# Output products in four 32-row tiles, half of their evictions split over two engines, and a list scheduler that writes the whole order

## The chip, the cores and the metric

One NeuronCore of a Trainium2 chip runs the whole program. The metric is the device time of one execution in microseconds (us), lower is better. Five engines work side by side, each through its own instructions strictly in the order in which the program lists them: PE (TensorE, matrix products; PEld is its loading of the stationary operand), DVE (VectorE), ACT (ScalarE), POOL (GpSimd) and SP, which here only starts DMA transfers. An instruction whose input is not there, or whose output buffer is not free yet, holds up everything behind it on its engine.

## What is computed

```python
# x: 4 x 12480 x 128, inducing: 32 x 128, w_in: 128 x 2048, w_out: 2048 x 128
def mab(q, kv):
    s = scale * (q @ kv.transpose(0, 2, 1))
    s = s - s.max(-1, keepdims=True)
    a = np.exp(s)
    a /= a.sum(-1, keepdims=True) + 1e-09
    return a @ kv
h = mab(I, x)          # 32 rows per batch, from all 12480 rows of x
y = mab(x, h)          # every row of x attends to those 32 rows
g = y @ w_in
out = np.maximum(0.01 * g, g) @ w_out
```

## The kernel before

The kernel has two paths. The one that runs, `fixed_sign_path`, uses that the rows of `h` differ little, so that every hidden unit has one sign for the whole batch. Then the two weight matrices fold with `h` into one 32 x 128 matrix M per batch, and the output is the attention weights of a row times M. A flag, computed at the end, says whether this held; the other path, which is as it was, would follow if not.

The 12480 rows of a batch are six groups of 2048 rows (J = 4 parts of 32 rows x K = 16) and a remainder of 192 rows, `RG`. There are four batches, so 24 groups and 4 remainders. Each group goes through two passes.

First pass: `load` brings 1 MB of x into `xr` (6 buffers). `turn` transposes it on PE in four quarters into `xT_ps` and copies each to `xT`. `first_scores` multiplies by the 32 inducing rows into `s_ps` and reads that out as `e`, with maxima. A step is two groups: `maxima` sets the shift, `weigh` takes the exponential (ACT) and transposes it to `ay` (DVE), `values` sums on PE into `h_ps`, `gather` adds that up.

Between the passes of a batch there is a chain: `inverse`, `normalise`, `hidden` (`H_ps`, `HT`), the leak on POOL (`G`), `fold` (`m_ps`), `spread` (`M_ps`). M is copied into `blocks`, block by block, so that 64 rows of the array serve two of the four parts J at a time: 64 x 258, which is two blocks of 128 columns and two columns of ones for the sums.

Second pass: `second_scores` (`s_ps` again) finds the largest magnitude (`low`), spreads it over the partitions with one more product (`low_ps`, `least`) and takes the exponential into `uT`. `output` then runs four times per group, once per quarter: two products of 64 rows x 258 columns into two banks of `po`, then on DVE the sums plus 1e-9 (`inv`, L1754), a reciprocal (L1755), and one multiplication that also moves 128 x 512 values to `osb` (L1756). `store` sends `osb` (2 buffers) out in four transfers of 256 KB.

PSUM has eight banks: `tp` (transposes and small products) two, `sc` (scores) one, `hp` (sums of values, and `m_ps`) one, `po` two buffers of two banks.

A loop over stages `s` writes the program: stage s transposes group s, takes the scores of s - 1, the second scores of s - 8, and the output of s - 9. The order on each engine is not quite that of the code, since the framework's own scheduler reorders what is written outside `manual_schedule`. In the fp32 products of the profile a matrix product is two MATMUL instructions, a transposition is one.

Of the kernel before, what the change touches and what calls it, by code (L numbers as in the profile page):

```python
# [11 lines left out]
I32 = mybir.dt.int32  # L12
# [1369 lines left out]

@with_exitstack
def fixed_sign_path(
# [33 lines left out]

    const = ctx.enter_context(tc.tile_pool(name="fconst", bufs=1))
# [12 lines left out]
    def value_ps(name):  # L1432
        return ps_h.tile([P, P], F32, tag="hp", name=name)

    def small(name, n=1, bufs=2):
        return sb.tile([P, n], F32, tag=name, name=name, bufs=bufs)
# [9 lines left out]
    blocks = [const.tile([P, 2 * P + 2], F32, tag=f"blocks{i}", name=f"blocks{i}") for i in range(2)]  # L1446
# [5 lines left out]
    hTs, sums_of, absolute, outs = {}, {}, {}, {}  # L1452
# [5 lines left out]
    def words(w):  # L1458
        return w.bitcast(I32).rearrange("p (n t) -> p n t", t=2)

    def setup():
# [13 lines left out]
        for blk in blocks:  # L1475
            nc.gpsimd.memset(blk, 0.0)
            for j in range(4):
                nc.gpsimd.memset(blk[32 * j : 32 * j + 32, 2 * P + j % 2 : 2 * P + j % 2 + 1], 1.0)
# [8 lines left out]
    def load(b, g, pieces=1):  # L1487
        J, K, rows, w = size(g)
        if g == RG:
            t = sb.tile([P, K, C], F32, tag="xrr", name="xrr", bufs=2)  # L1490
        else:
            t = sb.tile([P, K, C], F32, tag="xr", name="xr", bufs=6)
        src, n = rows_of(b, g), K // pieces
        for i in range(pieces):
            nc.sync.dma_start(t[:rows, n * i : n * i + n, :], src[:, n * i : n * i + n, :])
        xr[b, g] = t

    raws = []

    def load_weights(i):  # L1500
        raw = sb.tile([P, TOK, 2], I32, tag="osb", name="raw", bufs=2)
# [7 lines left out]
        raws.append(raw)  # L1509

    def convert(i):
        raw = raws[i]
        a = sb.tile([P, TOK], I32, tag="cv_a", name="cv_a", bufs=2)
        sign = sb.tile([P, TOK], I32, tag="cv_b", name="cv_b", bufs=1)
        tail = sb.tile([P, TOK], I32, tag="uT", name="cv_t", bufs=3)
        nc.scalar.mul(a.bitcast(F32), raw[:, :, 1].bitcast(F32), 2.0**-112)
        nc.vector.tensor_scalar(
            out=sign, in0=raw[:, :, 1], scalar1=-0x80000000, scalar2=None, op0=ALU.bitwise_and
        )
        nc.vector.scalar_tensor_tensor(  # L1520
            out=a, in0=a, scalar=3, in1=sign, op0=ALU.logical_shift_left, op1=ALU.bitwise_or
        )
        nc.scalar.mul(tail, raw[:, :, 0].bitcast(U32), 2.0**-29)
        if i < 4:
            dst, shape = w_in_sb[:, i].rearrange("p k r -> p r k").bitcast(I32), "p (r k) -> p r k"
            dst, a, tail = dst, a.rearrange(shape, k=16), tail.rearrange(shape, k=16)
# [4 lines left out]
    def turn(b, g, q, copy):  # L1531
        J, K, rows, w = size(g)
        n = min(K, 4)
        if q == 0:
            if g == RG:
                xT[b, g] = sb.tile([P, K, rows], F32, tag="xTr", name="xTr", bufs=3)
            else:
                xT[b, g] = sb.tile([P, K, rows], F32, tag="xT", name="xT", bufs=9)
        pt = turn_ps("xT_ps")
# [399 lines left out]
```

## Time and profile before

| | |
|---|---|
| device time, median of 3 runs | 373.02 us (372.03 to 373.57) |
| device time of the profiled execution | 367.05 us |
| its span, first to last instruction | 365.2 us |
| granted TensorE clock over the span | 0.867 of 2.4 GHz |
| moved by DMA | 55.80 MB, 153 GB/s over the span |

The profiled execution was 6 us shorter than the median of the timed ones. The profile's times are counted from the first instruction of the span. Busy times of an engine are the union of its instructions' times; a PE instruction's end is modelled, so the time from one product to the next is a better measure of PE than its length.

### The profile page before, as it was taken

Reading aid. Unit: us, or ns where it says so; the run is one execution under the profiler, and the core shown is the slowest. Engines: PE = TensorE matmul, PEld = TensorE weight load, DVE = VectorE, ACT = ScalarE, POOL = GpSimd, SP = SyncE. Lnnn points to the kernel's source line nnn. Section 1 sums busy time; section 2 is a strip of 40 time slices with the busy share of each in tenths; the row PEclk is TensorE's granted clock in tenths of the full one; section 3 lists DMA queues with packets and bytes.
Section 4 is the critical chain, followed back from the end, with each engine's and each line's share of the span. In section 5 each row is a group of like instructions: output and inputs, shape, how many; then the busy total and the mean of one; then the engine's idle time right before and its main releaser. Section 6 shows DMA issues by size and latency. Waiting matters only on the chain.

```text
span 365.2 us, 5886 instructions
## 1 busy us (share of the span) xinstructions
PE 277.1 (76%) x2275; PEld 144.0 (39%) x2275; DVE 189.4 (52%) x609; ACT 105.0 (29%) x221; POOL 17.1 (5%) x32
## 2 busy tenths in 40 slices
PE   4575968799989788887978886778977677685660
PEld 3343635455535353353534451433432222232420
DVE  1235553548555654546565744526754455646670
ACT  2454663535333351332422432041200100001000
POOL 2113230100000000000001000000001000000000
PEclk9679689999999999999987999898985598787555
DMA  7976685154582644048924096233613146356565
GB/s 237 426 270 191 213 300 188 56 226 120 128 278 58 151 196 118 0 117 325 290 88 117 7 260 206 44 83 79 156 32 83 37 120 150 79 133 149 126 162 115
DMA packets 20724, 55.80 MB, mean 153 GB/s; under 512 B 2352, under 2 KB 3536, under 8 KB 17872
## 3 DMA queue, kind: packets, MB, share of 16 engines
q1 hardware_dynamic: 20640, 55.32, 51.4%
q8 instruction: 20, 0.33, 0.4%
q14 instruction: 16, 0.13, 0.1%
q10 hardware_dynamic: 48, 0.02, 0.0%
HBM read 29.77 MB, written 25.56 MB: 152 GB/s over the span
## 4 chain that ended last, share of the span: by engine, by line
PE 60%; DVE 22%; ACT 6%; issue 4%; DMA 2%; SPq 1%; POOL 1%; DVEq 0%; POOLq 0%; ACTq 0%
PE s_ps L1549 18%; PE po L1748 16%; PE xT_ps L1541 10%; PE h_ps L1633 8%; DVE osb L1756 7%; DVE low L1720 4%; ACT xT L1544 4%; PE low_ps L1724 3%; DVE e L1566 2%; DMA raw<-in_moe_w_in_dram 2%; DVE ay L1610 2%; PE H_ps L1672 1%; DVE inv L1754 1%; PE m_ps L1695 1%; PE mx_ps L1582 1%
## 5 line engine op out<-in xcount | busy, mean ns | idle before, releaser
L1748 PE MATMUL po<-blocks,uT 64*128 64x258 f32 (+1 forms) x400 | 81.8, 497 | 27.3 <-DVE osb L1756 18.6
L1541 PE MATMUL xT_ps<-ident,xr 128*128 128x128 f32 x384 | 64.5, 309 | 7.3 <-ACT xT L1544 7.0
L1544 ACT COPY xT<-xT_ps 128x512 f32<-128x512 f32 x96 | 53.6, 585 | 53.5 <-PE xT_ps L1541 52.7
L1756 DVE TENSOR_TENSOR osb<-po,inv 128x512 f32<-128x512 f32 (+1 forms) x100 | 67.1, 686 | 1.9
L1748 PEld LDWEIGHTS po<-blocks,uT 64*128 64x128 f32 (+1 forms) x400 | 38.9, 217 | 73.0 <-issue 33.1
L1541 PEld LDWEIGHTS xT_ps<-ident,xr 128*128 128x128 f32 x384 | 47.9, 157 | 25.6 <-ACT xT L1544 14.3
L1735 ACT ACTIVATE uT<-s_ps,least 128x512 f32<-128x512 f32 (+1 forms) x28 | 17.8, 634 | 99.7 <-PE po L1748 51.4
L1549 PE MATMUL s_ps<-xT,hT 128*32 128x512 f32 x192 | 41.3, 644 | 4.2 <-DVE e L1566 3.1
L1754 DVE TENSOR_SCALAR inv<-po 128x4 f32<-128x4 f32 (+1 forms) x100 | 15.5, 155 | 42.7 <-PE po L1748 42.4
L1549 PE MATMUL s_ps<-xT,indT 128*32 128x512 f32 x192 | 32.5, 628 | 6.3 <-ACT xT L1544 5.9
L1566 DVE TENSOR_SCALAR_CACHE_REDUCE e<-s_ps 128x512 f32<-128x512 f32 (+1 forms) x28 | 17.4, 621 | 38.1 <-PE s_ps L1549 38.0
L1633 PE MATMUL h_ps<-xr,ay 128*32 128x128 f32 x768 | 32.6, 287 | 1.8 <-DVE ay L1610 1.7
L1633 PEld LDWEIGHTS h_ps<-xr,ay 128*32 128x32 f32 x768 | 24.3, 114 | 12.0 <-issue 7.4
L1720 DVE TENSOR_REDUCE low<-s_ps 128x1 f32<-128x512 f32 (+1 forms) x28 | 17.4, 623 | 19.9 <-PE s_ps L1549 19.9
L1724 PE MATMUL low_ps<-ident,low 128*128 128x128 f32 x56 | 14.9, 351 | 12.3 <-DVE low L1720 9.8
L1606 ACT ACTIVATE e<-e,nm 128x512 f32<-128x512 f32 (+1 forms) x28 | 18.3, 655 | 10.9 <-DVE nm L1585 10.9
L1724 PEld LDWEIGHTS low_ps<-ident,low 128*128 128x128 f32 x56 | 9.1, 204 | 28.9 <-DVE low L1720 21.0
L1610 DVE STREAM_TRANSPOSE ay<-e 128x512 f32<-128x512 f32 (+1 forms) x28 | 17.0, 626 | 5.0 <-ACT e L1606 5.0
L1755 DVE RECIPROCAL inv<-inv 128x4 f32<-128x4 f32 (+1 forms) x100 | 17.3, 173 | 2.3
L1601 ACT ACTIVATE al<-nm 128x1 f32<-128x1 f32 x8 | 2.4, 294 | 39.7 <-DVE lower L1587 36.6
L1726 DVE TENSOR_REDUCE least<-low_ps 128x1 f32<-128x128 f32 x28 | 8.0, 286 | 11.0 <-PE low_ps L1724 11.0
L1549 PEld LDWEIGHTS s_ps<-xT,hT 128*32 128x32 f32 x192 | 6.0, 111 | 15.6 <-DVE e L1566 6.4
(84 smaller groups left out, 138.6 us busy)
## 6 DMA issues: line engine op xcount, KB each, us to landing
out_dram<-osb SPq DMA_DIRECT2D x96, 256.0 KB, 4.4
xr<-in_x_dram SPq DMA_DIRECT2D x22, 1024.0 KB, 8.0
xr<-in_x_dram SPq DMA_DIRECT2D x8, 256.0 KB, 5.0
raw<-in_moe_w_in_dram SPq DMA_DIRECT2D x4, 512.0 KB, 8.6
raw<-in_moe_w_out_dram SPq DMA_DIRECT2D x4, 512.0 KB, 4.2
xrr<-in_x_dram SPq DMA_DIRECT2D x4, 96.0 KB, 8.3
out_dram<-osb SPq DMA_DIRECT2D x8, 48.0 KB, 1.7
ind<-in_inducing_dram ACTq DMA_DIRECT2D x1, 16.0 KB, 3.1
```

Source lines behind the costliest of these rows:

```text
L1541: nc.tensor.transpose(pt[:, k * rows : (k + 1) * rows], xr[b, g][:rows, 4 * q + k, :], ident[:rows, :rows])
L1544: copy(xT[b, g][:, 4 * q : 4 * q + n, :].rearrange("p k t -> p (k t)"), pt[:, : n * rows])
L1549: nc.tensor.matmul(ps[32 * j : 32 * j + 32, :w].rearrange("p (k r) -> p k r", r=32), lhsT, xT[b, g][:, :, 32 * j : 32 * j + 32], start=Tru ...
L1566: nc.vector.tensor_scalar(out=e[:rows], in0=sp[:rows, :w], scalar1=1.0, scalar2=None, op0=ALU.mult, op1=ALU.max, accum_out=rm[:rows],)
L1606: nc.scalar.activation(e[:rows, :w], e[:rows, :w], AF.Exp, bias=nm[:rows], scale=SCALE, accum_out=zg[:rows])
L1610: nc.vector.transpose(t[:rows].rearrange("p k m -> p (k m)"), e[:rows, :w])
L1633: nc.tensor.matmul(hp[32 * (k % 4) : 32 * (k % 4) + 32, :], t[:rows, k, :], rows_in[:rows, k, :], start=(i == 0 and k < 4), stop=(last[k % ...
L1720: nc.vector.tensor_reduce(out=low[:rows], in_=ps[:rows, :w], op=ALU.max, axis=AX.X, apply_absolute_value=True, negate=True)
L1724: nc.tensor.matmul(pl[:, :P], low.broadcast_to([P, P]), ident, start=True, stop=True)
L1748: nc.tensor.matmul(po[:m, h, : 2 * P + 2], part, blocks[b % 2][64 * h : 64 * h + 64, :], start=True, stop=True, tile_position=(64 * h, 0),)
L1754: nc.vector.tensor_scalar_add(inv2[:m], po[:m, :, 2 * P :][:, :, :2], 1e-9)
L1756: nc.vector.tensor_tensor(out=osb[:m, :, kk, :].rearrange("p (h j) c -> p h j c", h=2), in0=po[:m, :, : 2 * P].rearrange("p h (j c) -> p h ...
```

## The change

The formulas, the groups, the two passes and the transfers' sizes stay. Four things change.

1. `output` works on half a group with four tiles of 32 rows. M is copied once (`folded`, 128 x 129 with one column of ones) instead of four times, and every part J is a row tile of its own that writes into its own bank. A half group is 8 products of 32 rows x 129 columns, in four banks. `po` is now one buffer of four banks.
2. `inverses` takes the sums of a half group at once (128 x 8). `divided` evicts a half group in two pieces of 128 x 512: one is scaled on DVE as before, the other (`BY_COPY`) is copied unscaled by ACT and then multiplied in place by POOL.
3. `Plan` orders everything. Every piece of work is added with the engines that may do it, an estimated length, what it follows, the buffers that it takes and uses, and a rank. The scheduler repeatedly picks what can start soonest, and writes the program in the order of the starts that it worked out, under `manual_schedule`, so the framework does not reorder. A transposed quarter may be copied by ACT or by DVE, whichever the plan finds free.
4. The banks are dealt anew: `tp` two, `sc` two, `po` four; the sums of values and `m_ps` now take a `tp` buffer. `e` gets 4 buffers instead of 3, the weights have buffers of their own instead of those of `osb`.

```diff
+class Plan:
+    HANDOVER, LANDING, SWITCH, NEAR, STICK = 0.12, 2.0, 0.12, 0.1, 0.4
+    def ordered(self):
...
+                    at = max([free[engine]] + [from_op(a, engine) for a in after])
...
+                    start, order_rank = at, rank
+                    if mode is not None and mode != last_mode:
+                        start, order_rank = at + self.SWITCH, rank + self.STICK
+                    choices.append((start, order_rank, name, engine, length))
+            soonest = min(choices)
+            same = [c for c in choices if c[3] == soonest[3] and c[0] <= soonest[0] + self.NEAR]
+            start, _, name, engine, length = min(same, key=lambda c: (c[1], c[0], c[2:4]))
...
+    BY_COPY = ((0, 1), (1, 1))
-    ps_s = ctx.enter_context(tc.tile_pool(name="fps_s", bufs=1, space=bass.MemoryType.PSUM))
-    ps_h = ctx.enter_context(tc.tile_pool(name="fps_h", bufs=1, space=bass.MemoryType.PSUM))
-    ps_o = ctx.enter_context(tc.tile_pool(name="fps_o", bufs=2, space=bass.MemoryType.PSUM))
+    ps_s = ctx.enter_context(tc.tile_pool(name="fps_s", bufs=2, space=bass.MemoryType.PSUM))
+    ps_o = ctx.enter_context(tc.tile_pool(name="fps_o", bufs=1, space=bass.MemoryType.PSUM))
...
-        po = ps_o.tile([P, 2, TOK], F32, tag="po", name="po")
-        for h in range(2):
-            part = t[64 * h : 64 * h + 64, n * kk : n * kk + n, :].rearrange("p k r -> p (k r)")
-            nc.tensor.matmul(
-                po[:m, h, : 2 * P + 2], part, blocks[b % 2][64 * h : 64 * h + 64, :],
-                start=True, stop=True, tile_position=(64 * h, 0),
-            )
+        V["po", b, g, h] = po = ps_o.tile([P, 4, TOK], F32, tag="po", name="po")
...
+        for i in range(n):
+            flat = t.rearrange("p k r -> p (k r)")[:, m * (n * h + i) : m * (n * h + i) + m]
+            for j in range(J):
+                part = slice(32 * j, 32 * j + 32)
+                nc.tensor.matmul(
+                    po[:m, j, (P + 1) * i : (P + 1) * (i + 1)], flat[part], folded[b % 2][part, :],
+                    start=True, stop=True, tile_position=(32 * j, 0),
+                )
...
+        if step == "copy":
+            nc.scalar.copy(dst, src)
+            return
+        scale = inv[:m, j0:j1, :n].unsqueeze(3).broadcast_to([m, j1 - j0, n, C])
+        engine = nc.vector if step == "whole" else nc.gpsimd
+        engine.tensor_tensor(out=dst, in0=src if step == "whole" else dst, in1=scale, op=ALU.mult)
...
+            add(("C", b, g, q), {"ACT": 0.6 * f, "DVE": 0.7 * f}, lambda e, q=q: turned(b, g, q, e),
...
+    for emit in plan.ordered():
+        emit()
```

What this does to the order on PE is seen at two places. The names are those of the section on the kernel; `po` is the output product, `mx_ps` the product of `maxima`, and a row with xN is N products in a row. First, PE in the second half of the program, where both passes run. Before:

```order
L1748 MATMUL po<-blocks_84,uT 128x258 x8
L1549 MATMUL s_ps<-xT,indT 32x512
L1748 MATMUL po<-blocks_84,uT 128x258 x4
L1549 MATMUL s_ps<-xT,indT 32x512 x3
L1748 MATMUL po<-blocks_84,uT 128x258 x2
L1549 MATMUL s_ps<-xTr,indT 32x64 x3
L1748 MATMUL po<-blocks_84,uT 128x258 x2
L1582 MATMUL mx_ps<-rd,e_78 128x12
L1549 MATMUL s_ps<-xT,hT 32x512
L1748 MATMUL po<-blocks_84,uT 128x258 x2
```

And now, at a like place:

```order
L1863 MATMUL po<-folded_84,uT 128x129 x8
L1607 MATMUL xT_ps<-ident,xr 128x128 x12
L1863 MATMUL po<-folded_84,uT 128x129 x8
L1832 MATMUL low_ps<-ident,low 128x128
L1607 MATMUL xT_ps<-ident,xr 128x128 x4
L1627 MATMUL s_ps<-xT,indT 32x512 x4
L1607 MATMUL xT_ps<-ident,xr 128x128 x8
L1863 MATMUL po<-folded_84,uT 128x129 x8
L1665 MATMUL mx_ps<-rd,e_77 128x8
L1607 MATMUL xT_ps<-ident,xr 128x128 x8
L1627 MATMUL s_ps<-xT,hT 32x512 x4
```

Score products were cut in two by output products; now the four products of a group stand together, and transpositions stand between the halves of an output.

Second, PE from the last sum of values (`h_ps`) of the last batch on. Before:

```order
L1633 MATMUL h_ps<-xrr,ay 32x128 x2
L1652 MATMUL z_ps<-zn,e_78 128x1
L1549 MATMUL s_ps<-xT,hT 32x512
L1662 MATMUL hT_ps<-folds,hs 128x64
L1549 MATMUL s_ps<-xT,hT 32x512 x3
L1724 MATMUL low_ps<-ident,low 128x128
L1748 MATMUL po<-blocks_84,uT 128x258 x6
L1549 MATMUL s_ps<-xTr,hT 32x64 x3
L1748 MATMUL po<-blocks_84,uT 128x258 x2
L1724 MATMUL low_ps<-ident,low 128x128
L1672 MATMUL H_ps<-w_in_sb,hT 32x512 x4
L1549 MATMUL s_ps<-xT,hT 32x512 x4
```

And now (`z_ps`, `hT_ps`, `H_ps`, `m_ps` and `M_ps` are the products of the chain between the passes):

```order
L1723 MATMUL h_ps<-xrr,ay 32x128 x2
L1742 MATMUL z_ps<-zn,e_77 128x1
L1863 MATMUL po<-folded_83,uT 128x129 x8
L1755 MATMUL hT_ps<-folds,hs 128x64
L1766 MATMUL H_ps<-w_in_sb,hT 32x512 x4
L1627 MATMUL s_ps<-xT,hT 32x512 x4
L1863 MATMUL po<-folded_83,uT 64x129 x3
L1627 MATMUL s_ps<-xT,hT 32x512 x4
L1799 MATMUL m_ps<-w_out_sb,G 32x128 x16
L1832 MATMUL low_ps<-ident,low 128x128
L1810 MATMUL M_ps<-mc,e_77 128x128
```

Between the first product of the chain, `z_ps`, and `H_ps` stood eight output products of the batch before (four quarters), the second scores of a group and of a remainder, and three small products; now one half group and `hT_ps` stand there. From the last sum of values to the end the list before has the output of 38 quarters and two remainders; the list now has that of 13 halves and two remainders.

Third, PE at the very end. Before:

```order
L1724 MATMUL low_ps<-ident,low 128x128
L1748 MATMUL po<-blocks_85,uT 128x258 x6
L1549 MATMUL s_ps<-xTr,hT 32x64 x3
L1748 MATMUL po<-blocks_85,uT 128x258 x2
L1724 MATMUL low_ps<-ident,low 128x128
L1799 MATMUL v_ps<-ones,each 1x1
L1748 MATMUL po<-blocks_85,uT 128x258 x20
L1748 MATMUL po<-blocks_85,uT 64x258 x2
```

And now:

```order
L1832 MATMUL low_ps<-ident,low 128x128
L1863 MATMUL po<-folded_84,uT 128x129 x8
L1627 MATMUL s_ps<-xTr,hT 32x64 x3
L1832 MATMUL low_ps<-ident,low 128x128
L1863 MATMUL po<-folded_84,uT 128x129 x8
L1927 MATMUL v_ps<-ones,each 1x1
L1863 MATMUL po<-folded_84,uT 128x129 x48
L1863 MATMUL po<-folded_84,uT 64x129 x3
```

Before, ten quarters of two and a half groups and the remainder stood behind the last small product; now six halves, three groups, stand there in one run, each of which takes the only `po` buffer.

## Rows read from the trace of the kernel before

**Rows 1.** The page's head and part 1: busy time per engine, with shares of the span.

```profile
span 365.2 us, 5886 instructions
...
PE 277.1 (76%) x2275; PEld 144.0 (39%) x2275; DVE 189.4 (52%) x609; ACT 105.0 (29%) x221; POOL 17.1 (5%) x32
```

**Rows 2.** Windows: busy time (and count) per engine, PE's granted clock, DMA share, GB/s.

```profile
0.00:62.00 62.00, 42.05 (x386) 27.31 (x386) 24.59 (x67) 31.04 (x63) 12.58 (x26) 0.83 0.72 257
62.00:264.00 202.00, 170.55 (x1598) 90.50 (x1597) 112.30 (x375) 67.85 (x146) 3.43 (x5) 0.97 0.49 143
264.00:286.00 22.00, 15.07 (x89) 5.98 (x88) 11.12 (x38) 1.72 (x5) 1.05 (x1) 0.67 0.21 50
286.00:356.00 70.00, 49.41 (x204) 20.26 (x204) 41.43 (x131) 4.43 (x7) 0.00 (x0) 0.72 0.52 124
356.00:365.20 9.20, 0.00 (x0) 0.00 (x0) 0.00 (x0) 0.00 (x0) 0.00 (x0) 0.50 0.51 116
```

**Rows 3.** Groups on PE from 62 to 264 us: busy us, mean ns | idle before.

```profile
L1748 PE MATMUL po<-blocks,uT 64*128 64x258 f32 (+1 forms) x240 | 45.3, 452 | 9.8 <-DVE osb L1756 6.5 <-DVE inv L1754 3.3
L1549 PE MATMUL s_ps<-xT,hT 128*32 128x512 f32 x136 | 23.7, 603 | 3.1 <-DVE e L1566 3.1
```

**Rows 4.** Waits of PE from 62 to 264 us: total us, times, longest.

```profile
PE po L1748 <- DVE osb L1756: 6.5, 9, 1.2
PE low_ps L1724 <- DVE low L1720: 6.5, 14, 0.8
PE s_ps L1549 <- DVE e L1566: 3.4, 7, 0.8
```

**Rows 5.** Chain that ended last: start us, length us, what and how many instructions.

```profile
97.76 1.04 PE xT_ps L1541 x8
...
167.41 0.73 PE po L1748 x4
...
171.09 1.07 PE po L1748 x8
...
228.69 2.00 PE h_ps L1633 x64
...
286.25 1.26 PE po L1748 x4
```

**Rows 6.** Groups by form, whole span: busy us, mean ns | idle before.

```profile
L1756 DVE TENSOR_TENSOR osb<-po,inv 128x512 f32<-128x512 f32 x96 | 64.4, 687 | 1.9
L1544 ACT COPY xT<-xT_ps 128x512 f32<-128x512 f32 x96 | 53.6, 585 | 53.5 <-PE xT_ps L1541 52.7
L1541 PEld LDWEIGHTS xT_ps<-ident,xr 128*128 128x128 f32 x384 | 47.9, 157 | 25.6 <-ACT xT L1544 14.3 <-issue 8.5 <-DVE least L1726 1.3
...
L1755 DVE RECIPROCAL inv<-inv 128x4 f32<-128x4 f32 x96 | 16.7, 174 | 2.2
...
L1754 DVE TENSOR_SCALAR inv<-po 128x4 f32<-128x4 f32 x96 | 14.9, 155 | 41.8 <-PE po L1748 41.5
...
L1687 POOL TENSOR_TENSOR G<-HT,slope 128x512 f32<-128x512 f32 x4 | 4.2, 1047 | 161.2 <-DVE both L1781 117.6 <-DVE slope L1682 43.6
```

**Rows 7.** Instructions in order of time, 34.8 to 36.5 us: start, length, engine.

```profile
35.12 1.27 POOL L1529 TENSOR_TENSOR w_in_sb<-cv_a,cv_t 128x512 int32<-128x512 int32 x1 [0.69 <-DVE cv_a L1520]
...
35.62 0.80 DVE L1575 TENSOR_TENSOR rd<-rm,own 128x8 f32<-128x8 f32 x1
```

**Rows 8.** The instructions on tile rd: duration ns min/median/max.

```profile
L1575 DVE TENSOR_TENSOR rd<-rm,own x12: 155/167/795, 21.5 to 257.8; 128x8 f32<-128x8 f32 x8, 128x12 f32<-128x12 f32 x4
```

**Rows 9.** The chain again, from the last sum of values to the end.

```profile
262.93 0.80 PE h_ps L1633 x24
...
274.39 1.98 PE H_ps L1672 x8
...
355.18 0.68 DVE osb L1756
```

**Rows 10.** DMA issues of the page: KB each, median us to landing.

```profile
out_dram<-osb SPq DMA_DIRECT2D x96, 256.0 KB, 4.4
xr<-in_x_dram SPq DMA_DIRECT2D x22, 1024.0 KB, 8.0
```

More of the change, by code (lines that the diff above doesn't have):

```diff
@@ L1459, in words, with copying @@
         return w.bitcast(I32).rearrange("p (n t) -> p n t", t=2)
+    def copying(engine):
+        return nc.scalar.copy if engine == "ACT" else nc.vector.tensor_copy
     def setup():
@@ L1474, in setup @@
         )
[L1475 to L1478, printed above, removed]
+        for f in folded:
+            nc.gpsimd.memset(f, 1.0)
         pt = turn_ps("ind_ps")
@@ L1485, in rows_of, with load @@
         return x[b][at : at + 32 * J * K, :].rearrange("(p k) c -> p k c", k=K)
-    def load(b, g, pieces=1):
+    def load(b, g, i, pieces):
         J, K, rows, w = size(g)
[L1489 to L1498, printed above, removed]
+        if i == 0:
+            if g == RG:
+                xr[b, g] = sb.tile([P, K, C], F32, tag="xrr", name="xrr", bufs=2)
+            else:
+                xr[b, g] = sb.tile([P, K, C], F32, tag="xr", name="xr", bufs=BUFS["xr"])
+        t, src, n = xr[b, g], rows_of(b, g), K // pieces
+        nc.sync.dma_start(t[:rows, n * i : n * i + n, :], src[:, n * i : n * i + n, :])
     def load_weights(i):
-        raw = sb.tile([P, TOK, 2], I32, tag="osb", name="raw", bufs=2)
+        raws[i] = raw = sb.tile([P, TOK, 2], I32, tag="raw", name="raw", bufs=2)
         if i < 4:
@@ L1529, in convert, with turn @@
         nc.gpsimd.tensor_tensor(out=dst, in0=a, in1=tail, op=ALU.add)
-    def turn(b, g, q, copy):
+    def turn(b, g, q):
         J, K, rows, w = size(g)
[L1533 to L1539, printed above, removed]
-        for k in range(n):
+        V["T", b, g, q] = pt = turn_ps("xT_ps")
+        for k in range(min(K, 4)):
             nc.tensor.transpose(
@@ L1543, in turn, with turned @@
             )
-        copy(xT[b, g][:, 4 * q : 4 * q + n, :].rearrange("p k t -> p (k t)"), pt[:, : n * rows])
+    def turned(b, g, q, engine):
+        J, K, rows, w = size(g)
+        n = min(K, 4)
+        if (b, g) not in xT:
+            if g == RG:
+                xT[b, g] = sb.tile([P, K, rows], F32, tag="xTr", name="xTr", bufs=BUFS["xTr"])
+            else:
+                xT[b, g] = sb.tile([P, K, rows], F32, tag="xT", name="xT", bufs=BUFS["xT"])
+        copying(engine)(
+            xT[b, g][:, 4 * q : 4 * q + n, :].rearrange("p k t -> p (k t)"),
+            V.pop(("T", b, g, q))[:, : n * rows],
+        )
     def scores(ps, lhsT, b, g):
@@ L1892, in fixed_sign_path, with loading @@
-    verdict()
+    plan = Plan(BUFS | {"tp": 2, "sc": 2, "po": 1, "raw": 2, "cv_a": 2, "cv_b": 1, "xrr": 2, "folded": 2, "HT": 1, "hT": 2})
+    add = plan.add
+    def loading(b, g):
+        pieces = 4 if (b, g) in ((0, 0), (0, 1)) else 1
+        big = g != RG
+        tag = "xr" if big else "xrr"
+        for i in range(pieces):
+            add(("LD", b, g, i), {"DMA": (2.7 if big else 0.4) / pieces}, lambda _, i=i: load(b, g, i, pieces),
+                rank=b * NG + min(g, NG - 1) - BEFORE, takes=[(tag, b, g)] if i == 0 else [], uses=[(tag, b, g)])
@@ L1895, in induced_attention_then_leaky_ffn @@
+    for b in range(B):
+        for g in range(len(GROUPS)):
+            loading(b, g)
+            first_pass(b, g)
+            second_pass(b, g)
+        for p in range(len(STEPS)):
+            step(b, p)
+        middle(b)
+    for i in range(8):
+        weights(i)
+    add(("END",), {"DVE": 1.0}, lambda _: verdict(), after=[("CE", b) for b in range(B)], rank=1000)
+    setup()
+    for emit in plan.ordered():
+        emit()
 def induced_attention_then_leaky_ffn(tc, x, inducing, w_in, w_out, out):
```

486 lines of the change are left out of this document (288 added, 198 removed).

## The prediction

> **What bounds the kernel now.** I read the busy shares first: PE 76%, DVE 52%, ACT 29%, POOL 5% of 365.2 us [rows 1]. No engine is full, so the next view is the span cut where the work changes [rows 2]. Until 62 us only first passes run (H of the first batch starts at 62); until 264 both passes run; from 264 on no first pass is left. The three parts have different limits.
>
> From 62 to 264 us PE is busy 170.6 of 202 us at a granted clock of 0.97, which is nearly always the 2.4 GHz level; DVE is busy 112, ACT 68. PE sets the pace there, and its 31 us of idle time are short waits in a list: for `osb` to be evicted 6.5, for `low` 6.5, for `e` 3.4 [rows 4]. Of the busy time 45.3 us are output products, in 240 instructions, so 60 quarters at 0.75 us [rows 3].
>
> From 264 to 356 nothing is full: PE 64 of 92 us at clocks of 0.67 and 0.72, so partly at 1.2 GHz; DVE 53 [rows 2]. That is a list of hand-overs. The last sum of values ends at 263.7, but H starts only at 274.4 and the first output of the last batch at 286.3 [rows 5, 9]. The last 25 quarters then take until 355.9, 2.8 us each. 9.3 us follow in which the last transfers land.
>
> **The output product.** The trace has no product on 32 rows, so I price it by its neighbours. A quarter (two tiles of 64 rows, 258 columns, 4 instructions) takes 0.73 us alone, and two in a row take 1.07 [rows 5]: the second adds about 0.35 to 0.45. A half group is now 4 tiles x 2 products x 2 instructions = 16 instructions of 129 columns, four rounds of four tiles. The nearest row is the sum of values: four column tiles with 128 moving columns, 64 instructions in 2.00 us [rows 5], so 0.125 us a round and 0.50 us a half. Alone in the list, like the quarter, a half pays a start of about 0.25: 0.75. I take 0.62, with 0.50 and 0.75 as ends. Against that stand two quarters at 0.75 each: a half saves 0.9 us of PE.
>
> Dearer it would be if a 128-column weight load could not run beside a product on the same rows. A load's mean is 0.157 us [rows 6]; four rounds of 0.125 + 0.157 make 1.13. But eight transpositions, each with its own 128-column load on all rows, take 1.04 us, 0.13 each [rows 5]: less than one load alone, so loads and products do overlap there. [...]
>
> **The evictions.** DVE spends 155 + 174 + 687 = 1016 ns on a quarter [rows 6]. Per half it is the same once instead of twice (1.05 us, the sums being twice as many). ACT copies the other piece at about the 585 ns that it takes for 128x512 out of PSUM, and POOL scales it at about the 1047 ns of its own product of that shape with a broadcast operand [rows 6]. In the middle part 58 quarters and two remainders (-61 us) become 35 halves (+37), and about 24 of the 32 copies of `xT` that the plan gives to DVE (0.69 us each) add 17: DVE goes from 112 to 105 us, ACT from 68 to about 75. Neither becomes the limit if the part lasts over 150. POOL is cheap only if nobody waits for it: the scaling is followed by the store alone.
>
> One price stands in the way. While POOL ran its 1.27 us at 35.12, DVE's `rd`, which reads SBUF only, took 0.80 us and ended with it [rows 7]; its median is 0.167 [rows 8]. POOL will now be busy 39 x 1.05 = 41 us of the middle part, a quarter of it. About five DVE instructions per group read SBUF only (`ay`, two reciprocals, `rd`, sums); a quarter of them lose about 0.5 us: 0.6 us per group, 11 us of DVE's time, of which DVE's own slack hides half. It is within the idle time below; 0 and 20 are its ends.
>
> **The sum.** *First 62 us.* No output runs here. PE is idle for 20 us, 4 of them before the first rows arrive; ACT has 31 us, transposed copies and conversions. The plan lets DVE (25 us busy) copy too, gives scores a second buffer, and sends x ahead of the weights. I take half of the 16: 54. Ends: 48 and 62.
>
> *Middle, 202 us.* PE 170.6 - 45.3 + 36 x 0.62 + 1.4 (a group of second scores moves in: 23.7 us for 17, [rows 3]) = 149. Idle 31: the waits for `osb` and `e` have less behind them (half the DVE work per half, two score buffers), those for `low` stay, and new ones come with one `po` buffer and with POOL. I take 15: 164. Ends: 150 (nearly none) and 185 (idle as before, and the starts of more small runs).
>
> *Chain to the first output of the last batch, 22.5 us.* The list now has one half and one small product between `z_ps` and `H_ps`. The steps themselves, from the rows of [rows 9] and like instructions, are some 7 us, with 13 hand-overs at 0.1 and some at the lower clock 11. Ends: 9 and 22.
>
> *Twelve halves and a remainder, 69.6 us.* With one `po` buffer a half is: product, sums, reciprocal, multiplication, and only then the next. At 1.2 GHz, which this sparse stretch had, the product takes what a quarter takes there, 1.26 [rows 5]; then 0.16 + 0.18 + 0.69 + 0.3 of hand-overs: 2.6 us; at 2.4 GHz 2.0. The two `osb` buffers ask for about the same: a store is over 1 MB, its pieces land in 4.4 us [rows 10] after up to 3 us of issuing, so two groups cannot take less than 9.5 us. 12 x 2.6 = 31. Ends: 25 and 37. *The end* is 9.3 + 0.7, since POOL's scaling comes after the copy: 10.
>
> 54 + 164 + 11 + 31 + 10 = 270 us of span. The profiled execution was 367.05 for a span of 365.2; that makes 272. The median of the timed runs was 1.016 times that, so I predict **276 us**.
>
> **Rivals.**
>
> *The list stalls.* The plan assumes a hand-over of 0.12 us and 0.46 for a half, 0.9 for the scores; the scores take 1.04 and more. On strict lists each late item stops all behind it. For it: PE's idle time is made of such waits already. Against it: it is so before, too, and less work stands on DVE per output. If the middle keeps all its idle time and more, 187, and the first part 60: 300.
>
> *Four row tiles do not overlap* (weight loads first): 0.5 us more per half, 36 x 0.5 = 18 in the middle and 7 at the end: 301; if they ran wholly one after another, 16 instructions of 0.125, 1.4 more each, 342. Against it the 64-row quarters (0.4 us for the second) and the transpositions.
>
> *POOL holds DVE up.* If each of the 48 scalings stops something on the path for its whole 1.05 us: +50, 327. [...]
>
> *Slower than before: loads late behind stores.* SP's list is strict, and a store now waits for POOL's scaling at the end of a group; loads of x behind it wait too, and a load needs 8.0 us to land [rows 10]. With 18 groups loaded in the middle, each would have to reach PE 5.4 us late (97 / 18) to eat all that is won. The six `xr` buffers, loaded well ahead, speak against it, and PE's waits of before name no load.
>
> *Still faster:* clock at 2.4 GHz to the end, hardly any idle time in the middle, 48 in the first: 48 + 150 + 9 + 25 + 9.5, 247 after the same steps.
>
> **Chances.** Forecast, 247 to 292: 0.64. Stalls, 292 to 310: 0.15. Below 247: 0.09. Row tiles dearer or POOL in the way, 300 to 345: 0.09. Slower: 0.02; within half a per cent: 0.01. Half a per cent is about what these runs, 372.03 to 373.57, can tell from no change. The range 247 to 310 leaves out about two in ten; faster has 0.97, same 0.01, slower 0.02.
>
> **What would show it.** Right: the output products of a half start four at a time, some 0.11 us from round to round, and take 0.5 to 0.75 us; PE in the middle is busy over 88%, and the middle lasts 150 to 175 us; H of the last batch starts under 4 us after the last sum of values; the last halves follow each other at 2.0 to 2.6 us. Wrong: rounds further apart; long waits of PE for `xr`, `po` or `tp`; DVE's `ay` and reciprocals often near 1 us beside POOL; an end that waits for stores.

## The result, and the profile after

The changed kernel takes 268.02 us (median of 4 runs, 267.30 to 271.43) beside 372.52 us for the kernel before on the same chip (4 runs, 367.45 to 373.57). The ratio is 0.724, with a 95% interval from 0.713 to 0.736. Some executions of a program come out over 1.5% longer than its shortest, as the 271.43 us here; the ratios in this document leave such runs out, the medians do not.

The profiled execution took 267.3 us. Its page head and part 1, as in [rows 1]:

```profile
span 265.5 us, 6777 instructions
...
PE 201.0 (76%) x2667; PEld 131.0 (49%) x2667; DVE 168.5 (63%) x490; ACT 113.3 (43%) x232; POOL 65.6 (25%) x68
```

PE's busy share is what it was, 76%, but of a span that is 100 us shorter: PE itself has 76 us less to do. The windows, cut near the same events as [rows 2] (H of the first batch, the end of the last sum of values, the first output behind the last batch's M, the last eviction; that output begins at 216.8 us, so 0.5 us of the third row belongs to the fourth):

```profile
0.00:57.00 57.00, 42.90 (x433) 28.49 (x437) 35.36 (x85) 30.39 (x61) 11.45 (x16) 0.94 0.79 280
57.00:206.40 149.40, 131.03 (x1903) 86.22 (x1903) 107.56 (x327) 70.81 (x149) 39.56 (x38) 0.95 0.77 216
206.40:217.30 10.90, 9.22 (x120) 4.25 (x120) 7.87 (x21) 2.33 (x5) 2.09 (x2) 1.00 0.50 107
217.30:256.00 38.70, 17.88 (x228) 12.04 (x220) 17.60 (x59) 9.78 (x17) 12.49 (x12) 0.62 0.63 140
256.00:265.50 9.50, 0.00 (x0) 0.00 (x0) 0.10 (x1) 0.00 (x0) 0.00 (x0) 0.50 0.51 118
```

More than half of the gain, 52.6 us, is in the middle, and 39.5 of these are PE's busy time (170.55 to 131.03). Its groups there, to hold against [rows 3]:

```profile
L1607 PE MATMUL xT_ps<-ident,xr 128*128 128x128 f32 x236 | 35.6, 286 | 5.3 <-ACT xT L1619 4.6 <-DVE lower L1674 0.4
L1863 PE MATMUL po<-folded,uT 32*128 32x129 f32 x572 | 27.9, 309 | 9.7 <-DVE osb L1892 7.2 <-DVE zn L1709 2.3
L1723 PE MATMUL h_ps<-xr,ay 128*32 128x128 f32 x576 | 19.2, 290 | 0.0
L1627 PE MATMUL s_ps<-xT,hT 128*32 128x512 f32 x144 | 18.2, 598 | 0.0
L1627 PE MATMUL s_ps<-xT,indT 128*32 128x512 f32 x128 | 17.1, 599 | 0.4 <-ACT uT L1851 0.3
```

The output products went from 45.3 to 27.9 us, for 35 halves and two remainders where the middle held 58 quarters and two remainders. The second scores went from 23.7 to 18.2 though there are 8 instructions more, and the mean length of one is the same (603 and 598 ns). So what changed is not the instruction but how many run side by side.

The step between the batches is short now. In the chain of work that ended last, H of the last batch starts 1.9 us after the last sum of values, with one half group between them (10.7 us in [rows 9]):

```profile
203.87 2.52 PE h_ps L1723 x44
...
206.70 0.70 PE po L1863 x16
...
208.27 1.11 PE H_ps L1766 x8
```

At the end a half group takes longer than I had worked out. One of the last halves in the same view:

```profile
241.32 1.28 PE po L1863 x16
...
242.67 0.59 ACT osb L1888
...
243.29 0.18 DVE inv L1874
...
243.49 0.21 DVE inv L1875
...
243.73 0.70 DVE osb L1892
...
244.56 1.28 PE po L1863 x16
```

ACT's copy of one piece and DVE's work on the sums and the other piece do not run side by side. They follow each other, and the next product comes 3.24 us after this one. The waits from 217 to 256 us (total us, times, longest) have DVE's first work on the sums behind ACT's copy eleven times:

```profile
DVE inv L1874 <- ACT osb L1888: 17.2, 11, 2.1
```

### The profile page after: what moved, and what is told of

It reads as the page before. It is cut to its first block, busy times and chain, and to the rows that moved or that the text cites. A ratio compares the mean times of both kernels' runs of the same rounds, so it can differ in the third digit from the quotient of the medians.

```text
span 265.5 us, 6777 instructions
## 1 busy us (share of the span) xinstructions
PE 201.0 (76%) x2667; PEld 131.0 (49%) x2667; DVE 168.5 (63%) x490; ACT 113.3 (43%) x232; POOL 65.6 (25%) x68
## 4 chain that ended last, share of the span: by engine, by line
PE 46%; DMA 15%; DVE 15%; ACT 10%; issue 4%; SPq 4%; POOL 2%; ACTq 0%; DVEq 0%; POOLq 0%
PE xT_ps L1607 12%; DMA out_dram<-osb 11%; PE po L1863 11%; PE s_ps L1627 10%; PE h_ps L1723 7%; ACT osb L1888 6%; DVE osb L1892 5%; SPq L1905 4%; DMA raw<-in_moe_w_out_dram 3%; ACT xT L1619 2%; POOL osb L1892 2%; DVE inv L1874 2%; DVE inv L1875 2%; PE H_ps L1766 1%; DVE low L1825 1%
## 5 line engine op out<-in xcount | busy, mean ns | idle before, releaser
L1892 POOL TENSOR_TENSOR osb<-osb,inv 128x512 f32<-128x512 f32 x48 | 50.0, 1041 | 136.8 <-DVE inv L1875 53.5
L1863 PE MATMUL po<-folded,uT 32*128 32x129 f32 (+1 forms) x792 | 42.6, 332 | 26.0 <-DVE osb L1892 23.6
L1619 ACT COPY xT<-xT_ps 128x512 f32<-128x512 f32 x64 | 36.5, 586 | 40.1 <-PE xT_ps L1607 29.8
L1863 PEld LDWEIGHTS po<-folded,uT 32*128 32x128 f32 (+1 forms) x792 | 31.7, 213 | 43.1 <-issue 24.1
L1888 ACT COPY osb<-po 128x512 f32<-128x512 f32 x48 | 28.1, 585 | 54.7 <-PE po L1863 38.8
L1892 DVE TENSOR_TENSOR osb<-po,inv 128x512 f32<-128x512 f32 (+1 forms) x52 | 35.4, 681 | 8.8 <-ACT osb L1888 6.9
L1874 DVE TENSOR_SCALAR inv<-po 128x8 f32<-128x8 f32 (+1 forms) x52 | 8.6, 165 | 42.5 <-ACT osb L1888 32.9
L1619 DVE COPY xT<-xT_ps 128x512 f32<-128x512 f32 x32 | 21.6, 686 | 7.5 <-PE xT_ps L1607 6.8
L1851 ACT ACTIVATE uT<-s_ps,least 128x512 f32<-128x512 f32 (+1 forms) x28 | 17.7, 635 | 20.2 <-DVE least L1837 18.4
L1723 PE MATMUL h_ps<-xr,ay 128*32 128x128 f32 x768 | 25.6, 290 | 0.0
L1627 PE MATMUL s_ps<-xT,hT 128*32 128x512 f32 x192 | 24.4, 599 | 0.5 <-ACT uT L1851 0.5
```

Of the source, the lines that this page charges most:

```text
L1619: copying(engine)(xT[b, g][:, 4 * q : 4 * q + n, :].rearrange("p k t -> p (k t)"), V.pop(("T", b, g, q))[:, : n * rows],)
L1627: nc.tensor.matmul(ps[32 * j : 32 * j + 32, :w].rearrange("p (k r) -> p k r", r=32), lhsT, xT[b, g][:, :, 32 * j : 32 * j + 32], start=Tru ...
L1723: nc.tensor.matmul(hp[32 * (k % 4) : 32 * (k % 4) + 32, :], t[:rows, k, :], rows_in[:rows, k, :], start=(i == 0 and k < 4), stop=(last[k % ...
L1851: nc.scalar.activation(dst, src, AF.Exp, bias=least[:rows, b, g : g + 1])
L1863: nc.tensor.matmul(po[:m, j, (P + 1) * i : (P + 1) * (i + 1)], flat[part], folded[b % 2][part, :], start=True, stop=True, tile_position=(3 ...
L1888: nc.scalar.copy(dst, src)
```

## The experiments

The theory after this reading had three parts. The written order brings most of the time, partly by keeping PE's runs whole; the row tiles bring a smaller part; and late halves are long because the two readers of `po` stand in line. Its rivals were that the tiles bring most, that splitting the evictions does, and that POOL holds DVE up. This table gives the five parts of each span in us, cut in each trace at the events named above, with the output of a full group as the first output behind M; the times are medians of 4 to 6 runs, the ratios those to the kernel before on the same chip, with their intervals. In free, onlytiles and fixedbefore outputs of the batch before still stand behind the last M (5 halves, 4 halves and 4 quarters, each time with a remainder), so their column of halves holds more than the last batch.

| kernel | first | middle | chain | halves | end | span | time | ratio |
|---|---|---|---|---|---|---|---|---|
| again (the change once more) | 57.8 | 148.5 | 10.4 | 38.9 | 9.5 | 265.2 | 267.94 | 0.723 (0.718 to 0.728) |
| free | 57.5 | 188.6 | 13.2 | 73.1 | 9.6 | 342.0 | 342.73 | 0.918 (0.913 to 0.923) |
| fixedbefore | 65.6 | 230.1 | 19.4 | 55.1 | 9.2 | 379.4 | 379.07 | 1.016 (1.011 to 1.021) |
| onlytiles | 62.5 | 190.3 | 24.9 | 63.2 | 8.7 | 349.6 | 350.36 | 0.938 (0.931 to 0.945) |
| oldtiles | 55.7 | 159.9 | 11.6 | 47.9 | 9.0 | 284.1 | 287.22 | 0.772 (0.768 to 0.776) |
| cut | 64.1 | 154.5 | 10.4 | 40.7 | 9.4 | 279.0 | 278.77 | 0.755 (0.750 to 0.760) |
| dveonly | 56.9 | 163.9 | 10.9 | 44.0 | 8.8 | 284.5 | 286.73 | 0.765 (0.759 to 0.772) |
| noscale | 58.1 | 147.7 | 10.6 | 38.6 | 8.5 | 263.5 | 264.58 | 0.713 (0.709 to 0.717) |
| actcopies | 55.2 | 161.4 | 10.4 | 40.1 | 9.2 | 276.3 | 278.71 | 0.747 (0.739 to 0.755) |
| twotiles | 56.5 | 145.7 | 9.5 | 37.3 | 9.4 | 258.4 | 260.70 | 0.704 (0.700 to 0.708) |
| threestores | 52.1 | 150.7 | 9.2 | 31.3 | 10.2 | 253.5 | 259.62 | not given |
| warm | 53.2 | 151.9 | 11.2 | 31.6 | 10.4 | 258.3 | 258.72 | not given |

### Order or tiles

**free** takes the written order away from the changed kernel:

```diff
-        with tc.manual_schedule():
-            fixed_sign_path(tc, x, inducing, w_in, w_out, out, flag)
+        fixed_sign_path(tc, x, inducing, w_in, w_out, out, flag)
+        with tc.manual_schedule():
```

> The changed kernel with its list order given up again: the same tiles, the same split evictions, the same buffers, but the framework's own scheduler may move the instructions, as it could in the kernel before. If the written order brings the gain in the first part and the middle, their waits come back and the time is 300 us or more. The rival: the gain lies in the four row tiles, the split and the new buffers, and any scheduler would do; then 265 to 280 us.

**fixedbefore** does the reverse to the kernel before: `fixed_sign_path` moves into `manual_schedule`, so that its loops' own order holds.

> The kernel before with its instructions fixed in the order in which its own loops write them; nothing else differs. It parts two ways in which an order can bring time. If what hurts the kernel before is that the framework moved its instructions, fixing them gives some 350 us or less. If what hurts it is that nobody weighed the five engines against each other (the loops write a stage's work for one engine as a block), fixing the order brings nothing: 370 to 420 us, with PE idle for more than 53 us of the middle.

**onlytiles** gives the kernel before the row tiles, with the one `po` buffer of four banks that they write into, and nothing else of the change:

```diff
-        po = ps_o.tile([P, 2, TOK], F32, tag="po", name="po")
+        po = ps_o.tile([P, 4, TOK], F32, tag="po", name="po")
...
+                nc.tensor.matmul(
+                    po[:m, j, (P + 1) * i : (P + 1) * (i + 1)], flat[part], folded[b % 2][part, :],
+                    start=True, stop=True, tile_position=(32 * j, 0),
+                )
```

> The kernel before with the four 32-row tiles alone: halves of 2 x 512 elements of output, one po buffer of four banks instead of two of two, one copy of M instead of four, everything evicted by DVE; stage loops and scheduler as before. If my sum holds, a half takes 0.62 to 0.75 us of PE in the place of 1.5, some 25 to 30 us off PE in the middle, of which a part comes back as waits for the one buffer, and the last batch wins nothing before its halves, which then take about 3 us each: 330 to 350 us. If the tiles are the whole of the gain: below 300.

**oldtiles** puts the 64-row tiles back into the changed kernel, four products per half, with four copies of M:

```diff
-                    po[:m, j, (P + 1) * i : (P + 1) * (i + 1)], flat[part], folded[b % 2][part, :],
-                    start=True, stop=True, tile_position=(32 * j, 0),
+                    po[:m, 2 * i + j, : 2 * P + 2], flat[part], blocks[b % 2][part, :],
+                    start=True, stop=True, tile_position=(64 * j, 0),
```

> The changed kernel with the two 64-row tiles of before (block-diagonal M, 258 columns, four products per half), everything else as in the change, order and split too. If the list order brings most: the middle's 35 halves take about 0.5 to 0.8 us more each (17 to 28 us), the last twelve 0.8 us more each (10 us), and four copies of M for one lie on the last batch's chain (2 us): 290 to 305 us. If the tiles bring most: 320 or more.

The four come out as the order theory has them. Without the written order the changed kernel loses 75 us of its 104 (342.73); with the old tiles it loses 19 (287.22). To the kernel before, the tiles alone give 6%; 350.36 us is just above the range that I had for it. Fixing an order is worth nothing in itself: in fixedbefore PE waits for one item above all, in the middle:

```profile
PE low_ps L1724 <- DVE low L1720: 32.0, 19, 3.5
```

What counts is which order is fixed. In free, PE needs 156.1 us in the middle for 1808 instructions, in the changed kernel 131.0 for 1903. The scores, 272 instructions in both, are the largest part of that, 56.5 us for 35.3; the granted clock, 0.87 instead of 0.95, is another:

```profile
L1627 PE MATMUL s_ps<-xT,hT 128*32 128x512 f32 x144 | 28.3, 631 | 1.1 <-DVE e L1646 0.8 <-ACT uT L1851 0.3
L1627 PE MATMUL s_ps<-xT,indT 128*32 128x512 f32 x128 | 28.2, 737 | 4.0 <-ACT uT L1851 2.4 <-DVE e L1646 0.8 <-ACT xT L1619 0.7
```

oldtiles came out 3 us below its range. The halves of the middle cost it 42.2 us of PE against 27.9, so 0.4 us each, where I had expected 0.5 to 0.8.

### Scores in whole runs

The trace of the kernel before shows what a cut run costs. PE, in order of time (start, length, instructions):

```profile
101.22 1.05 PE L1549 MATMUL s_ps<-xT,indT 128*32 128x512 f32 x2
102.20 1.14 PE L1748 MATMUL po<-blocks,uT 64*128 64x258 f32 x8
103.27 1.06 PE L1549 MATMUL s_ps<-xT,indT 128*32 128x512 f32 x6
...
106.90 1.07 PE L1549 MATMUL s_ps<-xT,hT 128*32 128x512 f32 x8
```

The four products of a group lie in four column tiles. Eight instructions in one run take 1.07 us; the same eight, cut into two and six, take 1.05 and 1.06. That the framework's scheduler makes such cuts is seen in fixedbefore: in the loops' own order all 34 runs of the middle are whole, and the scores take 36.8 us there, 47.9 in the kernel before.

```profile
L1549 PE MATMUL s_ps<-xT,hT 128*32 128x512 f32 x136 | 18.7, 624 | 0.8 <-DVE e L1566 0.8
L1549 PE MATMUL s_ps<-xT,indT 128*32 128x512 f32 x136 | 18.1, 605 | 1.8 <-ACT xT L1544 1.4
```

Whole runs alone do not make that kernel faster, since PE waits for `low` instead. **cut** does the reverse to the changed kernel: in 19 places the fourth product stands behind PE's next work.

```diff
+        if ("S1", b, g) in cut:
+            scores(sp, indT, b, g, range(3))
+            rest["S1", b, g] = lambda: scores(sp, indT, b, g, [3])
...
+            if then < reader and names[then][0] in ("T", "O", "V", "L") and names[then][2:] :
+                cut.add(name)
+                behind[then] = name
     for n, emit in enumerate(emits):
         emit()
+        if n in behind:
+            rest.pop(behind[n])()
```

> The changed kernel with the scores of 19 of the 48 passes over a full group cut in two on PE: three of the four products together, the fourth behind the next work of PE, as the order of the kernel before often had it. Nothing is added or left out. In the kernel before, 8 instructions of scores in one run took 1.07 us, and 2 on their own took 1.05 as well. If PE's busy time in the middle fell by more than I predicted because the list keeps such runs whole, each cut costs about 1.05 us of PE; some 12 to 14 of the 19 lie in the middle, so its busy time grows by about 13 us and the whole time by 8 to 15: 276 to 283 us. The rival: a cut is hidden in PE's waits, or the loss before was in the waits alone; then less than 3 us more, 267 to 271.

It took 278.77 us, 10.8 more than the change, and 4.4% more by the two ratios. PE's busy time grew from 201.0 to 216.5 us, so 0.8 us for each cut. The theory holds in kind. The place differs from what I wrote: only 6.2 of the 15.5 us are in the middle, 6.7 in the first part (49.6 us busy there for 42.9). Six of the cuts lie before the first H, nine in the middle and four behind it, where I had 12 to 14 in the middle; and a fourth product that fell into a run of sums of values ran partly beside it (one of its instructions started at 66.51 us and took 0.59, the sums' next piece started at 66.57 and took 0.61).

### The evictions

**dveonly** leaves ACT and POOL out of the evictions:

```diff
-    BY_COPY = ((0, 1), (1, 1))
+    BY_COPY = ()
...
-                    add(("D", *key, h, t), {"DVE": 0.7 * f}, lambda _, h=h, t=t: divided(b, g, h, t, "whole"),
+                    add(("D", *key, h, t), {"DVE": 0.69 * f}, lambda _, h=h, t=t: divided(b, g, h, t, "whole"),
```

> The changed kernel with every piece of output evicted by DVE: no copies by ACT, no scaling by POOL, one plan made anew. In the trace of the change a late half goes po, ACT's copy, sums, reciprocal, DVE's eviction, one after another (3.25 us), so ACT's copy would save a half no time. If so, the last halves stay within 0.3 us of 3.25 us and the time grows only by what 24 us more of DVE in the middle make PE wait: 268 to 276 us. The rival, by the prediction's working (the two evictions of a half run side by side): 0.6 to 0.7 us more for each of twelve late halves and DVE behind in the middle too, 280 us or more.

It took 286.73 us, so my figure failed and the time lies where the rival had it, though not for the rival's reason. The reason that I gave held for the halves: the last ones follow each other at 3.17 us. Two multiplications on DVE take there what ACT's copy and one multiplication take in the change:

```profile
261.35 1.28 PE po L1863 x16
...
262.65 0.18 DVE inv L1874
...
262.85 0.21 DVE inv L1875
...
263.09 1.30 DVE osb L1892 x2
...
264.52 1.28 PE po L1863 x16
```

What I had set too low is the middle: 15 us longer, with DVE busy for 119.0 us and PE idle for 26.4 instead of 18.4. PE's granted clock is lower there, too (0.91 instead of 0.95), and the sums of values take 25.0 us instead of 19.2. The last part is 5 us longer, in its first two halves: DVE's eviction of the first waited for a store that landed at 235.8 us, and behind the product of the second two groups' second scores took 3.6 us, which take 1.9 in the change. The sharing is worth 19 us here (286.73 to 267.94), most of it where both engines have other work as well.

**noscale** leaves POOL's scalings out:

```diff
-                    add(("D", *key, h, t), {"POOL": 1.1}, lambda _, h=h, t=t: divided(b, g, h, t, "scale"),
+                    add(("D", *key, h, t), {"POOL": 1.1}, lambda _: None,
```

> The changed kernel without POOL's scalings: half of the output's columns pairs stay unscaled (sums instead of means) and everything else keeps its place. If POOL holds nothing up but the few DVE instructions that read two SBUF tiles (1.6 us in all for rd), the time stays within 2 us of the changed kernel's, less up to 1 us of the last scaling. If a scaling by POOL holds DVE for its length, as one of the rivals had it, some of the 43 scalings' 45 us come off: 230 to 258 us.

It took 264.58 us, 3.4 less than the change and a little more than I gave it; 1.0 of that is the end. So POOL is not in the way of much: the rival that would have cost 50 us is out. DVE's busy time fell by 0.7 us, from 168.65 (again) to 167.94. The only group of DVE in which I see POOL's scalings is `rd`: three of its twelve instructions took 0.57 us beside a scaling and 0.15 to 0.16 without. Its two longest, 0.8 and 0.7 us, are in both kernels, beside POOL's work on the weights. Over all, in again and in noscale:

```profile
L1655 DVE TENSOR_TENSOR rd<-rm,own 128x8 f32<-128x8 f32 (+1 forms) x12 | 4.4, 365 | 0.2
```

```profile
L1655 DVE TENSOR_TENSOR rd<-rm,own 128x8 f32<-128x8 f32 (+1 forms) x12 | 3.2, 263 | 0.2
```

**actcopies** gives all the transposed quarters to ACT:

```diff
-            add(("C", b, g, q), {"ACT": 0.6 * f, "DVE": 0.7 * f}, lambda e, q=q: turned(b, g, q, e),
+            add(("C", b, g, q), {"ACT": 0.6 * f}, lambda e, q=q: turned(b, g, q, e),
```

> The changed kernel with all transposed quarters copied by ACT, as in the kernel before, and the plan made anew; DVE copies none. If the first part's gain (62 to 57 us) comes from DVE's share of the copies, the first part goes back to 60 to 62 us, and with some copies more on ACT's path in the middle the time is 272 to 277 us. The rival: the first part's gain is that x is loaded ahead of the weights, and ACT has room; then 266 to 270 us.

Neither theory has it. The first part is not longer (55.2 us), so DVE's share of the copies is not what shortened it; but the middle is 13 us longer (278.71 us). PE waits for evictions there:

```profile
PE po L1863 <- DVE osb L1892: 11.2, 8, 2.0
...
PE po L1863 <- ACT osb L1888: 2.5, 4, 1.6
```

With 176 instructions on ACT instead of 149, an output's copy stands behind transposed quarters, and the multiplication behind the copy.

### The late halves

**again** is the changed kernel once more, on the chip on which dveonly, noscale and twotiles ran.

> The changed kernel once more, on the chip of the other three of this set: 267 to 269 us.

**twotiles** gives a half two PSUM tiles of two banks, one for DVE's eviction, one for ACT's copy, with sums of their own:

```diff
-        V["po", b, g, h] = po = ps_o.tile([P, 4, TOK], F32, tag="po", name="po")
+        V["po", b, g, h] = po = [
+            ps_o.tile([P, 2, TOK], F32, tag=f"po{i}", name=f"po{i}") for i in range(2)
+        ]
```

> The changed kernel with each half's output in two PSUM tiles of two banks (one for DVE's eviction, one for ACT's copy) instead of one of four, with the sums taken from each apart: 2 x 0.32 us of DVE per half for 0.36. If the waits between ACT's copy and DVE's sums come only from the two reading one tile, copy and eviction run side by side, and the last halves take about 2.6 us instead of 3.25: 7 to 8 us off, about 260. If the last halves are bound otherwise (the stores, the output buffers), or the added sums cost DVE what is won: 266 to 275 us.

It took 260.70 us, 2.7% less than the change on the same chip. In the trace in order of time ACT's copy of one tile now runs beside DVE's work on the other:

```profile
219.82 0.59 ACT L1891 COPY osb<-po 128x512 f32<-128x512 f32 x1 [0.80 <-PE po L1865]
219.96 0.18 DVE L1878 RECIPROCAL inv<-inv 128x4 f32<-128x4 f32 x1
220.18 0.69 DVE L1895 TENSOR_TENSOR osb<-po,inv 128x512 f32<-128x512 f32 x1
```

The late halves follow each other at 2.5 us, as the theory has it. Two things changed at once, though: each engine reads a tile of its own, and the sums of ACT's banks are no longer taken together with those of DVE's. Which of them DVE's wait came from was not tried apart. The last part as a whole lost only 1.6 us (38.9 to 37.3); the rest of the gain lies in the middle and the chain. In the last part the halves now run into the stores, six times, once for 4.5 us:

```profile
ACT osb L1891 <- DMA out_dram<-osb: 7.6, 2, 4.5
DVE osb L1895 <- DMA out_dram<-osb: 5.1, 4, 2.7
```

**threestores** adds a third output buffer to it, in the room that the raw weights had:

```diff
-    BUFS = {"xr": 6, "xT": 9, "xTr": 3, "e": 4, "er": 2, "ay": 4, "ayr": 2, "uT": 3, "uTr": 2, "osb": 2}
+    BUFS = {"xr": 6, "xT": 9, "xTr": 3, "e": 4, "er": 2, "ay": 4, "ayr": 2, "uT": 3, "uTr": 2, "osb": 3}
...
-        raws[i] = raw = sb.tile([P, TOK, 2], I32, tag="raw", name="raw", bufs=2)
+        raws[i] = raw = sb.tile([P, TOK, 2], I32, tag="osb", name="raw", bufs=BUFS["osb"])
```

> The kernel with the two output tiles per half (twotiles) and a third output buffer; the weights' raw data lie in these buffers again. In twotiles ACT and DVE wait 12.7 us for stores to free an output buffer after the last sum of values, with halves 5.4, 3.7 and 3.4 us apart where the others are 2.5 apart. If these waits stand on the chain: 3 to 6 us off, 254 to 258. If the stores' own rate binds the end, or the chain goes elsewhere: 259 to 262.

**warm** adds to that four transpositions behind each late half, to keep PE busy:

```diff
+        if b == B - 1 and g != RG:
+            pw = turn_ps("warm_ps")
+            for k in range(4):
+                nc.tensor.transpose(pw[:, k * P : (k + 1) * P], ident, ident)
```

> threestores with four transpositions of the identity matrix, read by nobody, behind each half of the last batch. In the last part of the changed kernel PE is busy less than half of the time and its clock falls to the 1.2 GHz level, where a half's product takes 1.25 us instead of 0.73. If busy PE keeps 2.4 GHz there, eight or nine halves become 0.5 us shorter: 3 to 5 us below threestores. If the clock falls all the same, the added work delays the halves by up to 0.3 us each, or nothing: 0 to 4 us above threestores.

The last part falls to 31.3 us in threestores, so the stores' buffers were what held it. The time does not follow clearly: the six runs took 254.4 to 259.8 us, the profiled one 255.3, so no ratio is given, and what the third buffer is worth in time stays open. The median, 259.62, is not told apart from that of twotiles, which is then the version that is shown to beat both kernels. warm took 258.72 (252.84 to 260.98), no better than threestores by this measure. In its profiled run, of 260.18 us, the added work did not hold the clock; its shortest run has no trace. Three stretches of the profiled run, one after the other (length, PE's busy time, ..., granted clock):

```profile
205.10:211.00 5.90, 5.60 (x38) 2.48 (x36) 3.38 (x11) 0.77 (x2) 1.04 (x1) 0.50 0.38 96
...
216.30:233.00 16.70, 14.41 (x188) 9.22 (x188) 13.79 (x52) 7.30 (x13) 6.24 (x6) 1.00 0.52 123
233.00:244.00 11.00, 9.28 (x82) 6.82 (x82) 5.85 (x25) 2.34 (x4) 4.16 (x4) 0.53 0.77 205
```

PE was busy for 86% of the time from 216.3 to 233.0, at a granted clock of 1.00, and then the clock came to 0.53 all the same (233.0 to 244.0 us), for four halves.

## Why the prediction was right, and where it was not

| part | before | predicted | measured |
|---|---|---|---|
| first | 62 | 54 (48 to 62) | 57.0 |
| middle | 202 | 164 (150 to 185) | 149.4 |
| chain | 22.5 | 11 (9 to 22) | 10.4 |
| twelve halves and a remainder (before: 34 quarters and two remainders) | 69.6 | 31 (25 to 37) | 39.3 |
| end | 9.3 | 10 | 9.4 |

The forecast of 276 us stood 8 us above the result. The span was forecast at 270 us and came out at 265.5. The rest lies in the step from the profiled execution to the median: I took 1.016 for it, as before, and it was 1.003 here (267.3 to 268.02). That the span came so near is in part luck, since the middle was 15 us too high and the halves were 8 too low. The parts shrank as forecast, with two differences in the mechanism: whole runs of scores, which I did not have in the sum, took some 11 us off PE's busy time in the middle (fixedbefore has 36.8 us of scores there for 47.9), and the two evictions of a late half, which I let run side by side, did not.

Of the signs that I had named, the rounds, the length of a half's product and the start of H came (0.11 us, 0.73 us, 1.9 us). Three were missed: PE was busy for 87.7% of the middle instead of over 88, the middle took 149.4 us instead of 150 to 175, and the last halves 3.25 us instead of 2.0 to 2.6.

**A wrong reading of before.** I took the outputs from 286.3 us on for those of the last batch, 25 quarters at 2.8 us each. But the remainder of the batch before, whose output follows that batch's last group, comes only at 305.47:

```profile
305.47 1.12 PE L1748 MATMUL po<-blocks,uT 64*64 64x258 f32 x4 [0.68 <-DVE inv L1754]
```

So the 69.6 us hold 10 quarters of the batch before, 24 of the last and two remainders, about 2.0 us a quarter, and the chain's 22.5 us end at the first output behind the last M. In the change only the last batch's outputs stand there, so a part of the 30 us won in this stretch is five halves and a remainder that the list does earlier. The forecast of 31 us does not rest on this: it was added up from the steps of twelve halves.

**The middle, 15 us too high.** The idle time was near (15 predicted, 18.4 measured). PE's busy time was not: 149 predicted, 131 measured. I left every product but the output's at what it took before. The scores of both passes went from 47.9 us (24.2 and 23.7) to 35.3, for 272 instructions in both; the group more of second scores, for which I added 1.4, was made up by a group less of first ones. The list keeps their column tiles in one run: 8 of the 34 passes over a group were cut into two and six instructions before and one is now, and nine times two passes stand in one run, which takes 1.9 us. cut shows the effect, at 0.8 us per cut, and fixedbefore, whose runs are whole but single, has 36.8 us for these 272. The rest is transpositions, 42.0 to 35.6 (270 instructions to 236: 34 moved to the first part), and sums of values, 22.9 to 19.2. The output was 5.6 us dearer than I had it, 27.9 instead of 22.3: a half takes 0.73 us from its first product to its last, near my upper end, since nearly all stand alone in the order.

**What the tiles save.** I set a half at 0.62 against two quarters at 0.75, 0.9 us saved. oldtiles gives 0.4 us of PE per half for the tiles; the other part comes from joining two quarters into one run, which took 1.07 us before too [rows 5].

**The last halves, 8 us too low.** I had 2.6 us for a late half at the lower clock (product, sums, reciprocal, multiplication, hand-overs) and took 2.6 for all twelve. At a granted clock of 0.50 a half takes 3.25, since ACT's copy (0.59 us and its hand-over) stands ahead of the sums. The twelve took 37.5 us in all, 3.1 each, since the first four ran at a granted clock of 1.00 and took 2.6; that is 6.3 more than 12 x 2.6, and the remainder behind them, which I had not counted, takes the other 1.8. twotiles shows 2.5 without the copy in the line, and threestores, with that and a third output buffer, the 31 for the whole part. That the copies unload DVE without shortening a half is seen in dveonly.

**The row tiles** overlap as argued. In the trace's single records the four of a round start 7 ns apart and the rounds, from the second on, 0.11 us; nothing of the load-first reading is seen.

**POOL** was priced at 11 us of DVE's time with ends 0 and 20. noscale puts it at 0.7 us of DVE and at most 3.4 of the whole. I had let five instructions per group be held; of these only `rd` was, three times of twelve (0.57 us each), and `ay` took 0.63 us on average with the scalings and without. The five were my estimate from the one long `rd` of [rows 7]; the rows of noscale show `rd` alone.

**The first part** came 3 us later than forecast. actcopies shows that its gain does not come from DVE's copies, and free (57.5 us) that it does not come from the fixed order. What is left, x ahead of the weights and the added buffers, was not tried apart. **The chain** was right to 0.6 us. Loads late behind stores, the rival on the slower side, were not seen: PE's waits in the middle name no load.

## What to carry to other kernels

Products that share the array by column tiles should stand together in the order: here one of four tiles alone took 1.05 us and the whole run 1.07, and the framework's scheduler cut such runs. Splitting an eviction over two engines unloaded the busier one, for about as much as the row tiles brought (19 us each, taken from the change); it shortened the single step only when each engine had a tile and sums of its own. When PE's idle share looks small, its busy time can still hold much that an order removes (156 us of the middle in free, 131 in the change, at granted clocks of 0.87 and 0.95): compare the length of a run, not the mean of an instruction.

## What the runs showed of the hardware

Each record of the granted clock in the traces of before and after (22 and 8) is 1.00 or 0.50 of full speed; the prediction and the expectation of warm write these two levels in GHz. In the change a half's product took 0.73 us at the one and 1.25 at the other. In warm the mean clock was 1.00 from 216.3 to 233.0 us, with PE busy for 86%, and 0.53 in the 11 us behind; from 205.1 to 211.0 us it was 0.50, with PE busy for 95%. What it follows was not settled. The rounds of a half, four row tiles with 129 columns each, are 0.11 us apart, and a round of the sums of values, four column tiles with 128 columns, takes 0.125 [rows 5]; the loads of the stationary operand, one for each of the 16 instructions of a half and 0.21 us long on average, added nothing to that which shows.
